# A fused attention and feed-forward kernel: another hand-written order for the first stage, other planned times and SBUF places behind it

## The chip, the cores and the metric

The kernel runs on one core of a Trainium2 chip. The metric is the time of one execution on the device in microseconds; of several runs the median is taken.

## The reference

Attention of 8 batches with 8 heads, 576 positions and 64 values a head. Heads 0 to 3 see the last 32 positions, heads 4 to 7 every fourth of the last 128. Its output is the x of a dense feed-forward network:

```
scores = q @ k.T / 8, masked: rel = pos_q - pos_k
  heads 0-3: 0 <= rel < 32        heads 4-7: 0 <= rel < 128 and rel % 4 == 0
attn = softmax(scores) @ v                      # (8, 8, 576, 64)
x = attn as (4608, 512)                         # 4608 tokens
y = gelu_exact(x @ w_in) @ w_out                # w_in (512, 2048), w_out (2048, 512)
```

Everything is float32 at the inputs and outputs.

## The kernel before

The tokens are worked in chunks of 512: chunk c is the first 512 positions of a batch, and the last 64 positions of all batches make chunk 8. Products are made in parts: a float32 operand is split into a high and a low part, and each product of two operands is three matmuls, so that the weights are unpacked at the start (`split`, `rest`, `high` and `join` of w0 to w15: VectorE and ScalarE make the high and low part of each column block f of the two weight matrices in SBUF, L275 to L312; `mid` is a second way for some of them).

The first stage computes the attention of chunks 0 and 1 and the whole feed-forward network of chunk 0 (`h0` to `h15`: x times w_in and GELU, L689 and L696 to L701; `o0` to `o15`: times w_out, L712) while the weights arrive. The second computes chunks 1 and 2 (`ffn(1, f)`, `ffn(2, f)`, L689 and L712, too), with the weights kept in SBUF. Meanwhile the unpacked weights and sums of them go to DRAM (`keep`, L736, into wd; sums made by GpSimd and VectorE, L831 to L855, into sd). The third stage (from 236 us) takes the other six chunks in pairs; two chunks together take seven block products for eight (Strassen's way, M1 to M7). It reads weights and sums back in pieces of 512 KB through a ring of five places (`ring_load`, L1073), each loaded when TensorE has used the piece before in that place. VectorE and ScalarE make the operands (L962 to L978 for x, L1164 to L1196 for h and GELU) and take the results from PSUM (L1202 to L1277).

The attention of the later chunks lies between the products. For pairs of heads (c, p) the steps are: load of q and k (L338), `scores` on TensorE (L375, L389), the lowest score and its exponent (`lowest_half`, L439 and L441), `softmax` on ScalarE (L510), `norm_half` and `turn_both` on VectorE (L446 to L457), eight small transfers `swap_keys` that move keys between partitions (L465, two for each r of 0 to 3), a load of v (L344), `av_four` on TensorE (L655) and `x_back` on VectorE (L668). The pair (c, 0) carries heads of p 0 and 1, (c, 2) those of p 2 and 3.

Three tables set the order. SCHEDULE is a hand-written list of tokens; each token advances the named piece of work by one instruction on the engine that its letter or its default gives (`:a` ScalarE, `:d` VectorE), and `plan:26` sends out all planned steps with a time below 26. All later work consists of numbered steps with a planned time in units (a product of 6 matmuls is one unit, 1.36 us, in the third stage), to which SHIFTED adds its own number; they are sorted and sent out between the products of TensorE:

```
    def add(at, rank, gen):
        steps.append((round(at + SHIFTED.get(len(steps), 0), 4), rank, len(steps), gen))
...
    def upto(pos):
        nonlocal at
        while at < len(steps) and steps[at][0] < pos - 1e-6:
            at_once(steps[at][3])
            at += 1
```

PLACE_OF names for each tile the SBUF place that it takes (w: 19 places of a weight or 1024 columns, xg: 12, go: 4, sm: 3, st: 5); a tile waits until all users of the place before it are done. Every engine takes its instructions in the order in which they are sent out, and SP issues all transfers, again in that order, so that a transfer whose condition is not met holds those behind it.

The steps that are spoken of: 12 is lowest_half of (2, 0); 60 turn_both of (3, 0), 61 to 64 its swap_keys, 65 its load of v, 66 its av_four; 135 and 300 are av_four of (4, 2) and (6, 0), 323 that of (6, 2); 248 is turn_both of (5, 0), 249 to 252 its swap_keys; 449, 453, 458 and 460 are VectorE's sums of x for one pair of chunks; 789 is a last sum of a result of the pair before, whose outputs are written by step 790; ring load n is step 497 + n. 

Of the kernel before, what the change touches and what calls it, by code (L numbers as in the profile page):

```python
# [116 lines left out]
    xg="""0 1 2 3 4 5 6 7 8 9 10 11 0 1 2 3 9 10 11 0 1 2 3 9 0 1 2 3 9 4 2 5 6 7 8 3 9 4 2 5 6 7 3 9 4 7 3 4 7 8 6 3 4 7 8 10  # L117
11 0 1 5""",
    go="""0 1 2 3 0 1 2 3 0 1 2 3 0 1 2 3 0 1 2 3 0 1 2 0 3 1 2 0 3 1 2 0 3 1 2 0 3 1 2 0 3 0 3 1 2 2 1 3 0 3 0 2 1 2 1 3 0 3 0
# [1363 lines left out]
```

## Time and profile before

| | |
|---|---|
| median of 3 runs | 825.4 us (825.24 to 826.22) |
| the profiled execution | 823.03 us |
| its span, from the first to the last instruction | 821.2 us |
| mean granted TensorE clock | 0.997 |
| TensorE busy | 798.8 us, 97% |
| VectorE busy | 610.8 us, 74% |
| ScalarE busy | 537.9 us, 65% |
| GpSimd busy | 65.0 us, 8% |

A view of the profile shows an execution's instructions on each engine with start and duration, and, for an engine that stood still, the instruction or transfer that released it. A line such as L465 is the line of the kernel that issued it; the names are those of the tiles (ps is PSUM, sm, st and turned are tiles of the softmax, ring the ring of weights). SPq is SP's queue. The line of releasers names the condition that came last by the profile.

### The profile page before, as it was taken

To read this page: it belongs to the slowest core of one execution; us is meant where nothing else is said; L and a number is where in the kernel's file an instruction comes from. 1 tells how busy PE (TensorE), PEld (TensorE's weight loads), DVE (VectorE), ACT (ScalarE), POOL (GpSimd) and SP (SyncE) were. 2 spreads that over 40 slices of the span, in tenths; PEclk is the share of its full clock that TensorE was granted. 3 is DMA by queue.
4 is the path that set the end of the run, shared out by engine and by line. 5 is a ranking of instruction groups with operands and counts; after the bars stand their busy time and mean duration, and the time that the engine had idled before them with its cause. 6 is when DMAs were issued, how large, how long until landed. Compare 5 with 4: busy or idle time off the path is not lost.

```text
span 821.2 us, 19943 instructions
## 1 busy us (share of the span) xinstructions
PE 798.8 (97%) x8354; PEld 652.8 (79%) x8354; DVE 610.8 (74%) x717; ACT 537.9 (65%) x1182; POOL 65.0 (8%) x80
## 2 busy tenths in 40 slices
PE   7899989999999999999999999999999999999997
PEld 5688878888787878888887788888888888888886
DVE  8889865799988879855767698846574987183848
ACT  7588855667677666776566776959775647444452
POOL 2000005633333000000000000000000000000000
PEclk9999999999999999999999999999999999999999
DMA  9998388997989988887987778966576687656564
GB/s 358 416 420 347 122 327 326 349 336 278 302 295 320 285 272 287 267 296 242 335 262 253 214 239 273 341 213 236 159 245 202 192 285 228 202 184 200 188 199 155
DMA packets 132073, 218.61 MB, mean 266 GB/s; under 512 B 7184, under 2 KB 107792, under 8 KB 125584
## 3 DMA queue, kind: packets, MB, share of 16 engines
q1 hardware_dynamic: 131840, 217.21, 77.6%
q8 instruction: 66, 1.08, 0.5%
q14 instruction: 23, 0.19, 0.1%
q10 hardware_dynamic: 144, 0.13, 0.0%
HBM read 167.51 MB, written 42.99 MB: 256 GB/s over the span
## 4 chain that ended last, share of the span: by engine, by line
PE 86%; DVE 5%; DMA 4%; issue 2%; SPq 2%; ACT 1%; DVEq 0%; ACTq 0%
PE ps L1145 62%; PE ps L689 9%; PE ps L712 8%; PE ps L389 3%; PE ps L655 2%; DMA ring<-sd 2%; SPq L465 1%; DMA turned<-turned 1%; DMA raw_qk<-qk 1%; DVE sums L841 1%; DMA v_sb<-v 1%; DVE g L701 1%; PE ps L612 1%; PE ps L601 1%; DVE sums L851 1%
## 5 line engine op out<-in xcount | busy, mean ns | idle before, releaser
L1145 PE MATMUL ps<-g,ring 128*128 128x512 f32 x1170 | 271.5, 391 | 1.6 <-ACT g_value L1178 1.6
L1145 PEld LDWEIGHTS ps<-g,ring 128*128 128x128 f32 x1170 | 218.4, 188 | 49.0 <-issue 2.1
L1145 PE MATMUL ps<-xc_T,ring 128*128 128x512 f32 x672 | 163.2, 391 | 0.0
L1145 PEld LDWEIGHTS ps<-xc_T,ring 128*128 128x128 f32 x672 | 125.5, 188 | 26.7 <-DVE xc_T L970 0.3
L1192 DVE TENSOR_TENSOR g<-g_value,g 128x1024 fp32r<-128x1024 f32 x85 | 103.0, 1220 | 51.6 <-ACT g L1191 51.5
L1191 ACT CAST g<-g_value 128x1024 fp32r<-128x1024 f32 x85 | 88.6, 1049 | 28.4 <-DVE g_value L1193 13.0
L1145 PE MATMUL ps<-xc_B,ring 128*128 128x512 f32 x432 | 106.7, 391 | 0.0
L689 PE MATMUL ps<-x,weight 128*128 128x512 f32 x384 | 94.6, 398 | 2.5 <-DVE weight L191 2.1
L1145 PEld LDWEIGHTS ps<-xc_B,ring 128*128 128x128 f32 x432 | 80.7, 188 | 17.0
L712 PE MATMUL ps<-g,weight 128*128 128x512 f32 x384 | 91.4, 392 | 0.3 <-issue 0.3
L689 PEld LDWEIGHTS ps<-x,weight 128*128 128x128 f32 x384 | 72.3, 191 | 19.0 <-DVE weight L191 2.5
L712 PEld LDWEIGHTS ps<-g,weight 128*128 128x128 f32 x384 | 71.4, 188 | 15.7 <-issue 0.5
L510 ACT ACTIVATE sm<-sm,st 128x64 f32<-128x64 f32 (+1 forms) x224 | 75.8, 341 | 10.1 <-DVE st L441 9.9
L831 POOL TENSOR_TENSOR whole<-weight 128x512 f32<-128x512 f32 x32 | 52.2, 1663 | 67.5 <-DVE sums L841 29.8
L1170 ACT COPY ps<-ps 128x512 f32<-128x512 f32 x28 | 16.0, 571 | 61.3 <-PE ps L1145 55.2
L1212 DVE TENSOR_TENSOR acc_C<-ps,acc_C 128x1024 f32<-128x1024 f32 (+1 forms) x40 | 39.9, 1006 | 16.9 <-PE ps L1145 16.3
L1166 ACT COPY u<-ps 128x512 f32<-128x512 f32 x56 | 32.6, 584 | 20.5 <-PE ps L1145 20.2
L510 ACT ACTIVATION_READ_ACCUMULATOR sm<-sm,st 128x1 f32 x224 | 42.3, 189 | 0.0
L696 ACT ACTIVATE gf<-ps 128x512 f32<-128x512 f32 x32 | 19.1, 597 | 25.6 <-PE ps L689 21.6
L701 DVE TENSOR_TENSOR g<-gf,g 128x512 fp32r<-128x512 f32 x32 | 26.1, 818 | 12.9 <-ACT g L189 12.7
L389 PEld LDWEIGHTS ps<-raw_qk 64*32 64x32 f32 x2304 | 26.3, 110 | 11.5 <-issue 8.7
L1202 ACT COPY ps<-ps 128x512 f32<-128x512 f32 x52 | 28.9, 570 | 9.4 <-PE ps L1145 7.7
(162 smaller groups left out, 959.5 us busy)
## 6 DMA issues: line engine op xcount, KB each, us to landing
ring<-sd SPq DMA_DIRECT2D x112, 512.0 KB, 4.7
ring<-wd SPq DMA_DIRECT2D x84, 512.0 KB, 4.7
v_sb<-v SPq DMA_DIRECT2D x17, 1024.0 KB, 6.2
raw_qk<-qk SPq DMA_DIRECT2D x32, 512.0 KB, 6.5
wd<-weight SPq DMA_DIRECT2D x16, 1024.0 KB, 10.5
sd<-sums SPq DMA_DIRECT2D x16, 1024.0 KB, 6.2
raw_w<-w SPq DMA_DIRECT2D x15, 1024.0 KB, 17.4
mid_w<-w SPq DMA_DIRECT2D x8, 1023.5 KB, 17.4
```

What stands on the lines that cost most here:

```text
L389: nc.tensor.matmul(s.sc[32 * r:32 * r + 32, h, c0:c0 + s.nk], x[:, q0:q0 + 32], x[:, k0:k0 + s.nk], start=s.c > 1, stop=s.c > 1 or u == NU ...
L510: nc.scalar.activation(t, s.sc[:, h, at:at + 2 * KB] if s.c < 2 else t, AF.Exp, bias=st[:, 0], scale=SCALE if s.c < 2 else -1.0, accum_out ...
L689: nc.tensor.matmul(bank, weights[f][:, t, cc * P:(cc + 1) * P], x[:, xx], start=n == 1 and i == 0, stop=n == parts and i == 2)
L701: nc.vector.tensor_sub(g[:, 1], gf, g[:, 0])
L712: nc.tensor.matmul(ps[:, O_BANK.get(c, 0) + d], weights[f][:, t, DM + d * P:DM + (d + 1) * P], gs[f][:, u], start=f == first and n == 0, s ...
L831: nc.gpsimd.tensor_add(to, x, y)
L1145: nc.tensor.matmul(ps[:, bank], lhs, rhs, start=start and i == 0, stop=i == 5, skip_group_check=True)
L1166: nc.scalar.copy(spare_tile[k, i], bank("a", i))
L1191: add(base + t, 4, run("a", lambda k=k, v=v: nc.scalar.copy(operand(k, 0, final), val(v, j))))
L1192: add(base + t1, 4, run("d", lambda k=k, v=v: sub(operand(k, 1, final), val(v, j), operand(k, 0, final))))
L1202: add(base + t, 2, run("a", lambda: nc.scalar.copy(ps[:, to], ps[:, of])))
L1212: plus(to, src, to)
```

## The change

SCHEDULE differs from the token `join12.0` on: the unpacking of weights 12 to 15, the attention of chunk 1, the last blocks of chunk 0 and the writes of the kept weights stand in another order. The numbers of SHIFTED are other ones for most steps, so that 856 of the 1855 steps of the whole plan, tokens and numbered steps together, come at another place in the order. PLACE_OF names another place for 155 of 338 tiles. No instruction is added or removed, and the operands, shapes and engines are the same but for a few copies. The core of the diff, with the lines that hold the steps named above:

```diff
--- before.py
+++ after.py
...
 
...
-    0: 4.6, 1: -52.55, 4: -17.45, 5: -18.9, 6: 9.25, 7: -47.3, 8: -19.75, 9: -0.95, 10: -1.05, 11: -22.65, 12: -32.75, 13: -1.25,
...
-    53: -0.85, 54: -2.65, 55: -4.05, 56: -2.6, 57: -3.7, 58: -1.35, 59: -2.9, 64: -1.05, 65: 5.1, 67: 1, 70: -0.65, 75: 1.25,
...
-    124: 5.7, 125: 9.1, 127: 7.4, 128: 10.5, 129: 10.65, 130: 16.05, 131: 14, 132: 10.5, 133: 10.05, 134: 22, 135: 11.8,
...
-    295: 14.8, 296: 12.15, 297: 10, 298: 8.3, 299: 7.15, 300: 7.25, 301: 20.55, 302: 10.45, 303: -34.15, 304: -2.25, 310: -2.45,
-    317: 5.3, 318: 9.65, 319: 6.15, 320: 5, 321: 9, 322: 6.6, 323: 6.45, 324: 9.25, 325: 10.5, 326: -16.4, 327: 2.55, 328: -6.3,
...
-    432: 1.85, 434: -5, 437: 9.85, 438: 10.55, 440: 9.4, 441: 6.1, 442: 6.2, 448: 11, 449: 14.45, 450: 12.55, 451: 14.9,
-    452: 14.3, 453: 6.3, 454: 6.45, 455: 4.6, 464: 7.2, 465: 10.9, 468: 14.8, 469: 15.95, 470: 16.8, 471: 10.2, 472: 10.15,
...
-    490: 8.25, 491: 2.7, 494: 8.9, 495: 8.45, 496: 4.65, 497: -11.1, 500: 3.65, 501: 4.35, 504: 2.75, 505: 6.65, 506: 6.1,
-    507: 3.45, 508: 6.3, 509: 3.75, 510: 4.3, 511: 1.75, 512: 1.5, 514: 4.05, 515: 3.95, 516: 3.85, 517: 1.7, 520: 5.35,
...
-    788: 40.85, 789: 25.3, 790: 40.4, 795: 2.8, 796: 2.25, 804: 2, 805: 2.85, 810: 2.6, 813: 1.8, 814: 1.55, 815: 2.65, 816: 2.05,
...
+    47: -0.7, 50: -2.6, 51: -2.1, 52: -0.9, 53: -0.7, 54: -2.3, 55: -3.2, 56: -3.3, 57: -4.5, 58: -1, 59: -2.85, 60: -2.65,
+    61: 2.25, 64: -0.65, 65: 0.6, 66: -0.25, 69: -2.15, 70: -0.5, 76: -0.35, 82: 3.45, 83: 5.7, 84: 8.85, 85: 6.2, 86: 6.8,
...
+    130: 17.85, 131: 15.05, 132: 9.85, 133: 8.75, 134: 24.75, 135: 13.6, 136: 13.55, 137: 16.25, 138: -28.05, 139: -301.1,
...
+    293: 10.25, 294: 12.3, 295: 11.4, 296: 15.05, 297: 14.6, 298: 7.95, 299: 8.5, 300: 9.45, 301: 15.9, 302: 20.25, 303: -19.65,
...
+    319: 11.5, 320: 9.9, 321: 8.05, 323: 7.6, 324: 5.3, 325: 8.55, 327: 5.45, 328: 16.6, 329: 10.65, 330: 6.75, 333: 5.75,
...
+    438: 8.65, 439: 11.7, 440: 13, 441: 4.3, 442: 6.35, 443: -2.7, 448: 16.75, 449: 24.85, 450: 12.4, 451: 13, 452: 16.4,
+    458: 8.7, 459: 7.25, 460: 5.7, 461: 5, 462: 4.15, 463: 6.9, 464: 11.25, 465: 12.7, 467: 20.55, 468: 11.8, 469: 16.1,
...
+    502: 0.95, 504: 4.75, 505: 4.55, 506: 3.3, 507: 1.8, 509: 3.75, 510: 5.25, 512: 2.5, 518: 3.9, 519: 5, 520: 6.3, 521: 4.95,
...
-x1.0 x1.1:d x1.1 w15 h8 h8:a join11.1 split10 h8 join12.0 w13 split10*2 join12.1 h9 scores1.2 scores1.3
-high10:a rest10*2 low1.2 low1.2:a o7 h9 exp1.2 split11 h9:d split11 h10 h9 exp1.2 split11 exp1.3 rest11 o8 rest11 exp1.3
-high11:a sums1.2:d sums1.2 o9 split12 h10 join13.0 v1.2 norm1.2:d split12 norm1.3:d split12 turn1.2 turn1.3 h11 h10:a
-rest12 turn1.3:a h10 turn1.2:a high12:d join13.1 rest12 av1.2 h11 split13 mid14 h11:a split13 h12
-h11 join15.0 w14 split13 o10 av1.3 h12 h12:a rest13 join15.1 h12 o11 rest13 high13:a x1.2:a split14 x1.2 x1.3:a keep0
-qk2.2 split14*2 x1.3 h13 qk2.3 plan:26 rest14*2 keep1 keep2 o12 plan:27 high14:d h13 split15 h13:a split15 keep3 h13 h14 plan:28 split15
-rest15*2 o13 plan:29 high15:a keep4 h14 h14:a h15 plan:30 h14 o14 plan:31 h15 h15:a h15 o15 store0.0:d store0.2:a store0.1:a store0.0 store0.2
-store0.3:d store0.3 store0.1 keep5 keep6 keep7
...
+split10 h8 join12.0 h9 w13 split10*2 join12.1 h9 scores1.2 scores1.3 high10:a rest10*2 low1.2 low1.2:a o7 o8 exp1.3
+exp1.2 h9:d split11*3 h9 o9 exp1.3 rest11 exp1.2 h10 sums1.2:d rest11 high11:a join13.1 sums1.2 split12 join13.0 v1.2
+norm1.3:d norm1.2:d h10 split12 turn1.3:a turn1.2 split12 h10:a rest12 turn1.3 high12:d mid14 h10 rest12 split13
+turn1.2:a h11 split13*2 av1.2 h11 keep0 h12 o10 h11 av1.3 rest13 h12 join15.1 w14 join15.0 h12 h11:a h12:a rest13
+high13:a split14 o11 keep1 split14 h13:a x1.2 x1.3:a split14 x1.3 h13 keep3 x1.2:a qk2.2 h13 qk2.3 keep2 rest14 high14:d
+rest14 plan:26 split15 plan:27 split15 o12 h14 h13 split15 plan:28 o13 rest15*2 plan:29 keep4 high15:a h14 h15 h14 h14:a
+h15:a h15 o14 h15 o15 store0.3:d store0.0:d plan:30 store0.0 store0.1 store0.3 store0.2 store0.1:a store0.2:a keep7
+keep6 keep5 plan:31
```

The lines of PLACE_OF differ in the same way in w, xg and go.

## Rows read from the trace of the kernel before

**Rows 1.** The page, part 1: busy us, share of the span, instructions.

```profile
PE 798.8 (97%) x8354; PEld 652.8 (79%) x8354; DVE 610.8 (74%) x717; ACT 537.9 (65%) x1182; POOL 65.0 (8%) x80
```

**Rows 2.** What TensorE waits for: us in total, times, longest.

```profile
PE ps L655 <- DMA turned<-turned: 2.1, 2, 1.6
PE ps L689 <- DVE weight L191: 2.1, 1, 2.1
PE ps L655 <- DMA v_sb<-v: 1.8, 1, 1.8
PE ps L1145 <- ACT g_value L1178: 1.6, 1, 1.6
PE ps L655 <- DMA ring<-sd: 1.3, 1, 1.3
...
PE ps L1145 <- DMA ring<-sd: 1.0, 1, 1.0
...
PE ps L712 <- issue: 0.3, 1, 0.3
```

**Rows 3.** Windows: us, busy of each engine, granted clock, DMA share, GB/s.

```profile
120.00:124.00 4.00, 4.00 (x12) 2.94 (x11) 2.28 (x4) 3.93 (x5) 0.00 (x0) 0.63 1.00 414
...
113.00:200.00 87.00, 84.93 (x1092) 69.35 (x1092) 69.02 (x79) 55.81 (x148) 38.76 (x46) 0.98 0.90 341
...
213.00:217.00 4.00, 3.85 (x138) 3.38 (x139) 4.00 (x4) 1.54 (x2) 2.02 (x2) 1.00 1.05 408
...
240.00:330.00 90.00, 86.97 (x1020) 70.99 (x1008) 77.34 (x86) 64.66 (x134) 6.88 (x4) 1.00 0.90 292
330.00:660.00 330.00, 326.96 (x3359) 268.13 (x3358) 232.64 (x261) 229.41 (x489) 0.00 (x0) 1.00 0.77 249
```

**Rows 4.** Timeline of VectorE, 113 to 121 us: start, us, line, tiles.

```profile
114.60 1.22 DVE L439 SCALAR_TENSOR_TENSOR sm<-ps,masks 128x1024 f32<-128x1024 f32 x1 [2.19 <-PE ps L389]
...
118.86 0.69 DVE L191 CAST weight<-raw_w 128x1024 fp32r<-128x1024 f32 x1
```

**Rows 5.** The chain that ended last: start, us, what.

```profile
100.50 2.94 PE ps L689 x12
...
119.60 4.58 PE ps L689 x12
...
206.51 6.59 DMA v_sb<-v
...
293.86 7.41 DMA ring<-sd
...
345.21 1.56 PE ps L655 x90
```

**Rows 6.** Timeline of SP, the queue that issues the transfers.

```profile
201.44 4.97 SPq L465 DMA_DIRECT2D turned<-turned  x8
...
256.02 0.58 SPq L1073 DMA_DIRECT2D ring<-wd  x1
256.65 0.68 SPq L1073 DMA_DIRECT2D ring<-sd  x1
...
292.50 0.53 SPq L1073 DMA_DIRECT2D ring<-wd  x1
...
338.52 5.01 SPq L465 DMA_DIRECT2D turned<-turned  x8
```

**Rows 7.** Timelines of TensorE (264, 303 us) and VectorE (326, 337 us).

```profile
264.74 1.08 PE L1145 MATMUL ps<-g,ring 128*128 128x512 f32 x4 [1.61 <-ACT g_value L1178]
...
303.04 2.20 PE L1145 MATMUL ps<-g,ring 128*128 128x512 f32 x9
...
326.21 1.29 DVE L1212 TENSOR_TENSOR acc_early<-ps,acc_early 128x512 f32<-128x512 f32 x2 [1.52 <-PE ps L1145]
...
337.21 1.25 DVE L457 STREAM_TRANSPOSE turned<-sm 128x1024 f32<-128x1024 f32 x1
```

**Rows 8.** Transfers: count, KB each, median us from issue to landing.

```profile
ring<-sd SPq DMA_DIRECT2D x112, 512.0 KB, 4.7
```

More of the change, by code (lines that the diff above doesn't have):

```diff
@@ L114 @@
     w="""0 1 2 3 4 5 6 7 8 9 10 11 12 13 14 15 16 17 18 1 3 2 5 6 7 8 9 10 13 11 14 18 16 17 3 2 6 7 9 14 18 11 3 17 10 0 7 17
-18 0 6 7 18 14 2 9 18 0 11 3 14 17 2 3 18 9 0 17 10 11 9 6 3 0 18 7 2 11 4 12 6 9 3 4 18 7 15 11 1 0 4 5 8 7 17 15 12
-14 11 18 6 13 16 12 17 1 11 1 5 16 16 5 17 5 9 11 5 9 10 18 9 0 18 10 11 9 18 0 11 18 0 10 9 5 11 0 10 5 11 18 0 5 10""",
-    xg="""0 1 2 3 4 5 6 7 8 9 10 11 0 1 2 3 9 10 11 0 1 2 3 9 0 1 2 3 9 4 2 5 6 7 8 3 9 4 2 5 6 7 3 9 4 7 3 4 7 8 6 3 4 7 8 10
-11 0 1 5""",
-    go="""0 1 2 3 0 1 2 3 0 1 2 3 0 1 2 3 0 1 2 3 0 1 2 0 3 1 2 0 3 1 2 0 3 1 2 0 3 1 2 0 3 0 3 1 2 2 1 3 0 3 0 2 1 2 1 3 0 3 0
-2 1 2 1 3 0 3 0 2 1 2 1 3 0 3 0 2 1 2 1 3 0 3 0 2 1 2 1 3 0 3 0 2 1""",
+18 0 7 6 14 2 9 18 17 3 11 2 7 14 10 17 11 18 7 2 3 7 0 6 9 18 2 11 4 7 10 12 18 2 0 4 6 9 18 15 11 1 5 8 6 12 4 17 18
+0 10 14 9 13 16 8 12 11 10 13 4 8 8 4 11 8 10 2 8 10 14 2 5 2 14 10 3 5 2 10 3 14 2 3 5 8 10 3 14 8 2 10 3 14 2""",
+    xg="""0 1 2 3 4 5 6 7 8 9 10 11 0 1 2 3 9 10 11 0 1 2 3 9 0 1 2 3 9 4 2 5 6 7 8 3 9 4 2 5 6 7 8 3 9 7 8 3 9 6 2 8 3 9 6 10
+11 0 1 4""",
+    go="""0 1 2 3 0 1 2 3 0 1 2 3 0 1 2 3 0 1 2 3 0 2 1 3 0 2 1 3 0 2 1 3 0 2 1 3 0 2 1 3 0 3 0 2 1 2 1 3 0 3 0 2 1 2 1 3 0 0 3
+2 1 1 2 0 3 0 3 1 2 1 2 0 3 3 0 1 2 1 2 0 3 0 3 1 2 1 2 0 3 0 3 1 2""",
     sm="""0 1 2 0 1 2 1 2 0 1 2 0 1 2 0 1 2 0 1 2 0""",
@@ L126 @@
 low0.0 high0.0:a rest0.0 v0.0 rest0.0 low0.0:a scores0.2 exp0.0 low0.1 split0.1 fill split0.1 low0.1:a scores0.3
-sums0.0:a split0.1 exp0.1 mid1 sums0.0 low0.2 exp0.1 low0.2:d norm0.0:d exp0.2 turn0.0 w1 sums0.1:d fill*3 sums0.1 norm0.1:d
-low0.3 exp0.2 low0.3:d split0.1 turn0.1 half0.0.1:d half0.0.0:d v0.2 half0.1.1:a half0.1.0:a fill*2
-sums0.2:d sums0.2 norm0.2:d exp0.3 mid2 av0.0 turn0.2 exp0.3 rest0.1*2 high0.1:d w2 x0.0:a x0.1:a sums0.3:d sums0.3 norm0.3:d
-x0.0 x0.1 h0.0 turn0.3 h0.1 half0.2.0:a half0.2.1:a half0.3.1:a half0.3.0:a split1*3 qk1.0 av0.2 high1:a rest1*2 qk1.1 h1.0 h1.1
@@ L131 @@
-x0.2:a x0.3:a x0.2 x0.3 h0.2 h0.3 split2 h0 mid3 h1.2 w3 h1.3 scores1.0 burn*45 h0:a split2*2 high2:a rest2*2 h0 h1 h1:a h2 scores1.1
-split3 w4 mid5 split3 h1 o0 split3 rest3 h2 mid4 h2:a rest3 low1.0 low1.0:a
-exp1.0 o1 high3:d w5 exp1.0 h2 h3 split4 exp1.1 mid6 split4*2 exp1.1 o2 rest4 high4:a w6 rest4 h3
-split5*2 h4 w7 h3:a split5 sums1.0:a h3 high5:a rest5 o3 w8 rest5 h4 h4:a split6 join7.0 h4 w11 h5 split6 sums1.0
-join7.1 split6 norm1.0:d high6:a w9 o4 rest6*2 h5 h5:a split7 join8.0 mid9 h5 h6 split7 norm1.1:a split7 v1.0 join8.1
@@ L136 @@
-rest7 turn1.0 turn1.1 rest7 o5 high7:a split8 h6 qk1.2 split8 h6:a split8 turn1.0:a w10 h7 turn1.1:a h6 join11.0 rest8
-high8:a rest8 qk2.0 av1.0 split9 h7 split9 qk1.3 join10.0 split9 h8 av1.1 w12 h7:a h7 high9:a rest9 join10.1 x1.0:a qk2.1 rest9 o6
-x1.0 x1.1:d x1.1 w15 h8 h8:a join11.1 split10 h8 join12.0 w13 split10*2 join12.1 h9 scores1.2 scores1.3
-high10:a rest10*2 low1.2 low1.2:a o7 h9 exp1.2 split11 h9:d split11 h10 h9 exp1.2 split11 exp1.3 rest11 o8 rest11 exp1.3
-high11:a sums1.2:d sums1.2 o9 split12 h10 join13.0 v1.2 norm1.2:d split12 norm1.3:d split12 turn1.2 turn1.3 h11 h10:a
@@ L145 @@
-store0.3:d store0.3 store0.1 keep5 keep6 keep7
+sums0.0:a split0.1 exp0.1 mid1 sums0.0 low0.2 exp0.1 low0.2:d norm0.0:d exp0.2 turn0.0 w1 sums0.1:d fill*3 sums0.1
+norm0.1:d low0.3 exp0.2 low0.3:d split0.1 turn0.1 half0.0.1:d half0.0.0:d v0.2 half0.1.1:a half0.1.0:a fill*2 sums0.2:d
+sums0.2 norm0.2:d exp0.3 mid2 av0.0 turn0.2 exp0.3 rest0.1*2 high0.1:d w2 x0.0:a x0.1:a sums0.3:d sums0.3 norm0.3:d x0.0
+x0.1 h0.0 turn0.3 h0.1 half0.2.0:a half0.2.1:a half0.3.1:a half0.3.0:a split1*3 qk1.0 av0.2 high1:a rest1*2 qk1.1 h1.0
@@ new lines @@
+h1.1 x0.2:a x0.3:a x0.2 x0.3 h0.2 h0.3 split2 h0 mid3 h1.2 w3 h1.3 scores1.0 burn*45 h0:a split2*2 high2:a rest2*2 h0 h1
+h1:a h2 scores1.1 split3 w4 mid5 split3 h1 o0 split3 rest3 h2 mid4 h2:a rest3 low1.0 low1.0:a exp1.0 o1 high3:d w5
+exp1.0 h2 h3 split4 exp1.1 mid6 split4*2 exp1.1 o2 rest4 high4:a w6 rest4 h3 split5*2 h4 w7 h3:a split5 sums1.0:a h3
+high5:a rest5 o3 w8 rest5 h4 h4:a split6 join7.0 h4 w11 h5 split6 sums1.0 join7.1 split6 norm1.0:d high6:a w9 o4 rest6*2
+h5 h5:a split7 join8.0 mid9 h5 h6 split7 norm1.1:a split7 v1.0 join8.1 rest7 turn1.0 turn1.1 rest7 o5 high7:a split8 h6
@@ new lines @@
+qk1.2 split8 h6:a split8 turn1.0:a w10 h7 turn1.1:a h6 join11.0 rest8 high8:a rest8 qk2.0 av1.0 split9 h7 split9 qk1.3
+join10.0 split9 h8 av1.1 w12 h7:a h7 high9:a rest9 join10.1 x1.0:a qk2.1 rest9 o6 x1.0 x1.1:d x1.1 w15 h8 h8:a join11.1
+split10 h8 join12.0 h9 w13 split10*2 join12.1 h9 scores1.2 scores1.3 high10:a rest10*2 low1.2 low1.2:a o7 o8 exp1.3
+exp1.2 h9:d split11*3 h9 o9 exp1.3 rest11 exp1.2 h10 sums1.2:d rest11 high11:a join13.1 sums1.2 split12 join13.0 v1.2
+norm1.3:d norm1.2:d h10 split12 turn1.3:a turn1.2 split12 h10:a rest12 turn1.3 high12:d mid14 h10 rest12 split13
```

101 rows, old and new, of the table SHIFTED are left out of this document.

## The prediction

> **What bounds the kernel now.** I read the busy times first. TensorE has work in 798.8 us of a span of 821.2 us, and VectorE, the next, in 74% [rows 1]. No other engine can be the bound on average, so nothing that this change does to them pays unless it shortens the 22.4 us in which TensorE stands still (821.2 - 798.8). Second, the list of what TensorE waits for [rows 2]. A good part of it is the start of the kernel (attention of chunk 0, up to 80 us), which the new order does not touch, and some of it lies behind the last product. The rest, in time of the span, is seven stalls: one wait of 2.1 us for a weight, 2.1 us in two waits for turned keys, 1.8 us for a load of v, 1.6 us put down to a g value, 1.3 us and 1.0 us for loads into the ring, and 0.3 us of issue. Together they are 2.1 + 2.1 + 1.8 + 1.6 + 1.3 + 1.0 + 0.3 = 10.2 us, and this is what the change can take, with what follows from them. Third, the windows: in both long stretches up to 330 us, 113 to 200 and 240 to 330, the DMA engines are busy 0.90 of the time [rows 3], so transfers there cannot simply be moved ahead. Fourth, the chain and the timelines of the queues, to see who made each of the seven late.
>
> **The weight (117.5 us).** In VectorE's order the lowest-score step of the pair (2,0), step 12 (L439, L441), stands ahead of `rest14` (L300, L302), and it needs scores that end just before 114.60; VectorE is idle for 2.19 us before it and then needs until 118.86 to reach `high14`, for which `h14` waits [rows 4]. After the stall the granted clock is 0.63 over 120 to 124 us, between its two levels of 1.2 and 2.4 GHz [rows 3], and the 12 matmuls of `h14` take 4.58 us where the 12 of another product behind an attention block take 2.94 [rows 5]: 1.64 us more. In the new SCHEDULE `rest14 high14 rest14` stand ahead of `plan:26`, which means ahead of step 12 for VectorE, and weight 14 goes to a place that split14 itself frees. Then VectorE uses its idle 2.19 us and weight 14 is there some 2 us before TensorE wants it: -2.1 - 1.64 = -3.7 us. In exchange `high15` now runs on ScalarE behind seven pieces of softmax; adding up that queue I find it about 0.35 us late for `h15`: +0.35.
>
> The Trainium skill, page "TensorE: Matmul & The Clock Gate", section on HAM oscillation, says that a TensorE left waiting between bursts of matmuls starts the next burst at the lower clock, and pays for it at every such wait. If that held for each of the stalls of 1 us and more here, another five times 1.64 us would come back, and the time below would be 8.2 us lower. The trace doesn't agree: the clock is 1.00 in the 4 us behind the 1.8 us wait, and 1.00 over 240 to 330 us, where three more stalls lie [rows 3]. So I take this gain once.
>
> **v of pair (3,0) (211 us).** The eight swaps of keys (L465) wait for the turn, go out at 201.44 over 4.97 us, and the load of v stands behind them; it goes out at 206.51 and takes 6.59 us [rows 5, 6]. In the new numbers load_v (step 65) loses 4.5 units and stands ahead of the swaps, and the turn (step 60) loses 2.65. The matmuls that need it (step 66) come 0.25 units earlier, 2.72 us on TensorE, with over 2 us of room left: -1.8.
>
> **The ring (263, 293 us) and the keys (306, 432, 471 us).** Loads of the ring stand in SP's queue in pairs that are out of order: load 10 waits for TensorE and is issued at 256.02, load 9 behind it at 256.65 [rows 6], though the place of load 9 was free earlier. With the 7.41 us of a neighbour [rows 5] it lands at about 264.1, close to where the stall ends that the list puts down to the g value (264.74, [rows 7]). Steps 506 and 507 change from 6.1 and 3.45 to 3.3 and 1.8, which sets load 9 ahead: -1.6. Loads 19 and 20 (steps 516, 517) are the same, from 3.85 and 1.7 to none: -1.0. The matmuls on (4,2) and (6,0) (steps 135, 300) are moved back by two products, 2.72 us, the latter's turn comes some 2.5 us earlier, and (6,2) (step 323) moves back by one product while its swaps go ahead of the next ring load: -2.1 - 1.3. The 0.3 us of issue I count as gone with the order around it: -0.3. Sum of what goes: 3.7 + 1.8 + 1.6 + 1.0 + 2.1 + 1.3 + 0.3 = 11.8 us.
>
> **What the new order adds.** No instruction is added or removed, except that by the order of exponential and GELU on ScalarE I count 38 table loads for 42; ScalarE waits for others at most of these points, so I price that at nothing. The matmuls of the products are the same and in nearly the same order. What can cost is a step that comes too late.
>
> First, 131 to 240 us. The lowest and turn steps of chunk 2 are re-sorted among VectorE's sums for the ring. VectorE is busy 69.0 of the 87 us to 200 us [rows 3], so most slips are absorbed. Of several places the margin by my sums is 0 to 2 us (matmuls on (2,2), the x of chunk 2, (2,0) whose turn now waits for a place that GpSimd frees). Below: 0. Above: four places late by one operation of 1.22 us [rows 4], 4.9. I take one operation: +1.2.
>
> Second, 303 us. Ring load 21 was issued at 292.50 for matmuls at 303.04, 10.5 us ahead [rows 6, 7]; step 518 gets 3.9 units, and load 21 now stands behind four swaps that wait for a turn; its lead comes to 5.6 us. A neighbour took 7.41 us to land, the median of ring loads is 4.7 [rows 5, 8]. So 0 to 1.8 us; I take +1.0.
>
> Third, 345 us. Eight swaps for (5,0) start at 338.52, behind the turn (1.25 us from 337.21), over 5.01 us, and the matmuls on them began at 345.21, with 0.2 us to spare [rows 5 to 7]. Step 789 loses its 25.3 units and is now in VectorE's queue ahead of this turn, steps 449 and 458 gain units and are too, while steps 453 and 460 are out of the way: three operations for two between VectorE's last wait (326.21, [rows 7]) and the turn. One operation of some 1.15 us, less the 0.2: +0.95. If none of VectorE's idle time before 326 absorbs anything, three operations are late, and the cost is 3.5; if the swaps land faster, 0.
>
> Fourth, ring load 133 (643 us) gets behind four swaps in the same way, with a lead of 4.4 us against the median of 4.7: +0.5, between 0 and 1.5. And eight further places, from 328 to 737 us, where VectorE or ScalarE have up to 1 us more in their queue than before; both idle a quarter of the time or more, so +0.7 over all, between 0 and 3.
>
> Sum of additions: 0.35 + 1.2 + 1.0 + 0.95 + 0.5 + 0.7 = 4.7 us. Net 11.8 - 4.7 = 7.1 us.
>
> **The rivals.** (a) The DMA engines take it back. With seven stalls gone TensorE is up to 10 us ahead in the third stage, and every load is wanted that much earlier, while the DMA engines are busy 0.90 of the time up to there [rows 3]. Ten loads that miss by 0.7 us each give back all of it: 825. For it speaks that the ring loads near 290 us took 7.41 where the median is 4.7; against it, that after 330 us the share falls to 0.77, and that a load's issue waits for TensorE to free its place, so that both move together. The Trainium skill, page "DMA: Bandwidth & Descriptors", section on issuing engines, says that transfers run on the same 16 engines and interleave whoever issues them, so a load that is moved ahead delays another. The row of 0.90 agrees; by that rule alone the two ring stalls and the one for v would only change place, and 4.4 us of the gain would be gone.
>
> (b) Nearly full gain: if landings are at their medians, the additions shrink to under 2.5 us. 825.4 - 9.3 to 825.4 - 11.8: 813.6 to 816.1.
>
> (c) Slower. The keys for (5,0) are the one place where one queue holds up everything: SP's. If the turn is late by three operations and two outputs of the finished pair ahead of the swaps wait as well, all loads behind them on SP are late too: ring loads 36 to 39, each wanted 2.7 us after the other. It costs more than the 11.8 us only if the swaps go out about 15 us late (11.8 plus the other additions of 3.8, less 0.2 of slack), that is, if step 789 waits for a place or an operand that comes that late; at 17 us the time is about 827. I see no such operand in the numbers of the change.
>
> (d) The order of SP could be right and the first term wrong: if `h14` still waits for its weight, 3.7 us less gain, 822.
>
> **How the numbers follow.** The profiled execution took 823.03 us, of which 821.2 are span; the median of the runs is 825.4, 2.4 above it. Seen from the profiled one the sum is 823.03 - 7.1 = 815.9; on the median's footing, which is what will be compared, 825.4 - 7.1 = 818.3. A difference of 0.2% is 1.65 us, about what a measurement of this kernel can tell from none. My chances: the forecast (816.2 to 821.5) 0.56; (b) 0.15; (d) and the like, a smaller gain of 1.7 to 3.9 us, 0.11; (a) within 1.65 us of before 0.10; slower, by (c) or a sum of small stalls, 0.08. Faster: 0.56 + 0.15 + 0.11 = 0.82. For the range I leave out the last 0.08 and about half of (a) above, and the lowest half of (b) below: 814.8 to 824.6.
>
> **What would show it.** In the new profile: VectorE's `rest14` before L439 and no wait of TensorE for L191 near 117 us, with a clock of 1.00 over 120 to 124; the load of v ahead of L465's eight; ring loads from sd in the order of their use, and no wait at 263 and 293; new waits, if any, for turned keys near 340, and for the ring near 300 and 635. TensorE's idle time should fall from 22.4 to about 17 us. I am wrong if waits for DMA sum to as much as before, if the clock drops at another place, or if a wait of more than 3 us stands anywhere behind 113 us.

## The result and the profile after

The changed kernel takes 815.7 us in the median (815.06 to 818.61, 4 runs) where the kernel before took 825.32. The ratio is 0.9896, with a 95% interval of 0.9862 to 0.9929, so it is faster by 0.7 to 1.4%. A second measurement, beside experiments, gave 816.18 us and 0.9913 (0.988 to 0.9946). Over both, 12 runs of the changed kernel have a median of 815.7 us, and the 79 runs of the kernel before that were taken beside the experiments one of 822.8: 7.1 us. (Each measurement by itself gives 9.6 and 6.6 us.)

The profiled execution of the changed kernel is the slowest of its four runs, 818.61 us with a span of 816.7. Its busy times, against [rows 1]:

```profile
PE 801.0 (98%) x8354; PEld 653.2 (80%) x8354; DVE 609.3 (75%) x717; ACT 533.7 (65%) x1178; POOL 62.6 (8%) x80
```

TensorE now stands still for 816.7 - 801.0 = 15.7 us instead of 22.4. What it still waits for (us in total, times, longest), against [rows 2]:

```profile
PE ps L1146 <- DMA ring<-wd: 2.6, 1, 2.6
...
PE ps L390 <- DMA raw_qk<-qk: 1.8, 4, 0.6
...
PE ps L656 <- DMA turned<-turned: 0.4, 1, 0.4
```

All seven stalls of [rows 2] are gone or small: no weight, no v, no g value, 0.4 us of turned keys. What is left of any size behind 113 us is one new wait of 2.6 us for a load into the ring, beside 0.4 us of the waits for raw_qk and 0.2 us for ScalarE. The windows, against [rows 3] (us, busy time of PE, PEld, DVE, ACT, POOL with counts, granted clock, DMA share, GB/s):

```profile
113.00:200.00 87.00, 86.46 (x1103) 70.40 (x1103) 67.53 (x81) 58.24 (x151) 35.82 (x46) 1.00 0.85 316
...
240.00:330.00 90.00, 90.00 (x1000) 73.48 (x999) 82.36 (x88) 66.62 (x138) 5.91 (x4) 1.00 0.92 306
330.00:660.00 330.00, 327.08 (x3346) 267.85 (x3345) 230.21 (x258) 222.66 (x473) 0.00 (x0) 0.99 0.77 245
...
120.00:124.00 4.00, 3.97 (x17) 2.95 (x17) 1.97 (x3) 3.98 (x14) 1.50 (x8) 1.00 1.02 430
...
506.00:510.00 4.00, 2.66 (x6) 2.15 (x7) 2.70 (x5) 0.00 (x0) 0.00 (x0) 0.61 1.07 379
...
545.00:550.00 5.00, 5.00 (x173) 4.42 (x166) 1.40 (x2) 3.10 (x6) 0.00 (x0) 0.78 0.39 118
```

TensorE is busy in all of the 90 us from 240 to 330 where it was in 86.97, and VectorE does 82.36 us of work there for 77.34, although the DMA engines are as full as before (0.92 for 0.90). From 120 to 124 us the clock is 1.00 instead of 0.63. But it is low at two new places: behind the new wait (0.61 over 506 to 510 us) and from 545 us on, where TensorE had no idle time at all. This execution is 3.5 us above the fastest run, whose mean clock was 0.999 where this one's was 0.996; (1 - clock) times the span is 0.8 us there and 3.3 us here, so the clock is 2.5 of the 3.5 us.

The place of the weight, on VectorE and then ScalarE (start, us, engine, line, operation, tiles), against [rows 4]:

```profile
112.31 0.68 DVE L301 TENSOR_SCALAR spare<-raw_w 128x1024 uint32<-128x1024 uint32 x1
112.91 0.68 DVE L192 CAST weight<-raw_w 128x1024 fp32r<-128x1024 f32 x1
113.51 1.22 DVE L303 SCALAR_TENSOR_TENSOR weight<-raw_w,spare 128x1024 fp32r<-128x1024 uint32 x1
114.64 1.22 DVE L440 SCALAR_TENSOR_TENSOR sm<-ps,masks 128x1024 f32<-128x1024 f32 x1
...
121.82 1.10 ACT L190 CAST weight<-raw_w 128x1024 fp32r<-128x1024 f32 x1
122.94 1.28 ACT L697 ACT_TABLE_LOAD   x1
```

`rest14`, `high14` and the second `rest14` (L301, L192, L303) run from 112.31 to 114.73, and the lowest-score step (L440) only then, at nearly the same time as before. `high15` ends on ScalarE at 122.92. The chain, against [rows 5]:

```profile
117.51 2.72 PE ps L690 x12
...
122.97 3.01 PE ps L690 x12
...
507.34 13.90 PE ps L1146 x54
```

`h14` (117.51) and `h15` (122.97) begin without a wait in the list; `high15` ended 0.05 us before `h15` began. The scores of (2,2) and (2,3), which stood at 124 us between the last products of chunk 0, are now at 134.32. SP's queue, against [rows 6]:

```profile
493.99 5.02 SPq L466 DMA_DIRECT2D turned<-turned  x8
...
499.69 0.58 SPq L1074 DMA_DIRECT2D ring<-wd  x1
...
330.81 5.03 SPq L466 DMA_DIRECT2D turned<-turned  x8
```

The swaps for (5,0) begin at 330.81 and the matmuls on them at 337.66, 6.9 us later; it was 6.7 before, and there is no wait. The new wait stands at 507.34: eight swaps for (8,0) go out from 493.99 on, and the ring load behind them only at 499.69; the chain has 7.51 us for it.

### The profile page after: what moved, and what is told of

Read it like the earlier page. It is cut to its first block, busy times and chain, and to the rows that moved or that the text cites. A ratio compares the mean times of both kernels' runs of the same rounds, so it can differ in the third digit from the quotient of the medians.

```text
span 816.7 us, 19941 instructions
## 1 busy us (share of the span) xinstructions
PE 801.0 (98%) x8354; PEld 653.2 (80%) x8354; DVE 609.3 (75%) x717; ACT 533.7 (65%) x1178; POOL 62.6 (8%) x80
## 4 chain that ended last, share of the span: by engine, by line
PE 84%; DVE 7%; DMA 4%; ACT 2%; issue 1%; SPq 1%; DVEq 0%; ACTq 0%
PE ps L1146 62%; PE ps L690 8%; PE ps L713 7%; PE ps L390 3%; DMA raw_qk<-qk 2%; PE ps L656 2%; ACT sm L511 1%; DMA v_sb<-v 1%; DVE sums L842 1%; DMA ring<-wd 1%; DVE sums L852 1%; PE ps L613 1%; PE ps L602 1%; SPq L466 1%; DMA turned<-turned 1%
## 5 line engine op out<-in xcount | busy, mean ns | idle before, releaser
L1175 DVE TENSOR_TENSOR g_value<-ps,u 128x512 f32<-128x512 f32 x28 | 19.2, 688 | 25.4 <-PE ps L1146 23.6
```

## The experiments

The twelve runs were taken in three groups, each on a chip of its own and beside the kernel before: `e1` to `e4` (before: 824.12 us), `a_again` and `u1` to `u3` (822.76), `e6` to `e8` and `u4` (822.33). Between groups the ratios are compared. `e1` to `e3` and `e6` to `e8` make a part of the change in the kernel before; `u1` to `u4` undo one part of it in the changed kernel; `e4_fix` goes beyond it. Each profile is one execution. Numbers in the diffs are entries of SHIFTED. Changes of the places that only follow from a moved step are left out of the diffs.

**The ring loads alone, in the kernel before (`e1_ring`).**

```diff
-    506: 6.1, 507: 3.45, 516: 3.85, 517: 1.7
+    506: 3.3, 507: 1.8
```

> The kernel before with four numbers changed, so that ring load 9 stands ahead of load 10 and load 19 ahead of load 20 in SP's queue. Theory of the order in the queue: TensorE's waits of 1.6 us near 263 and 1.0 us near 293 are gone and nothing takes their place but some tenths at the keys of (4,2) near 306: 1.6 to 2.6 us faster than before. Rival, that the DMA engines set the pace there: a later load or transfer misses instead, the waits for DMA keep their sum and the time stays within 0.8 us of before.

Measured: 828.67 us (822.6 to 832.39), ratio 1.0058 (1.0033 to 1.0083): slower, which neither theory had expected. TensorE's waits in its profile (start, us, tiles, and in brackets idle time and releaser) and, behind the last "...", SP's queue:

```profile
267.00 12.64 PE L1145 MATMUL ps<-g,ring 128*128 128x512 f32 x48 [1.99 <-ACT g L1191]
...
294.86 1.61 PE L1145 MATMUL ps<-xc_T,ring 128*128 128x512 f32 x6 [1.26 <-DMA ring<-sd]
...
257.93 0.58 SPq L1073 DMA_DIRECT2D ring<-wd  x1
258.56 0.67 SPq L1073 DMA_DIRECT2D ring<-sd  x1
```

The edit does more than it was meant to. By the planned times load 9 is now ahead of load 10, but both are also ahead of load 8 (step 505: 6.65 here, 4.55 in the change), and load 19 is ahead of 17 and 18 (steps 514 and 515: 4.05 and 3.95 here, none in the change). TensorE needs these loads in the order of their numbers, which the change gives them. So the transfer at 258.56, behind load 10 (257.93), is load 8; it takes 8.1 us to land, to 266.7, and TensorE goes on at 267.00. The list names a cast of g on ScalarE instead, but under `e7_ringkeys`, which has the same four numbers, TensorE goes on while that cast still runs. The wait at 294.86 is for load 17, sent out behind 19. The keys of (4,2) cost 1.93 us for 0.46. This run therefore does not show what loads in the order of their use would bring.

**The weight alone, in the kernel before (`e2_weight`).**

```diff
-qk2.2 split14*2 x1.3 h13 qk2.3 plan:26 rest14*2 keep1 keep2 o12 plan:27 high14:d h13 split15
+qk2.2 split14*2 x1.3 h13 qk2.3 rest14 high14:d rest14 plan:26 keep1 keep2 o12 plan:27 h13 split15
```

> The kernel before with rest14, high14, rest14 ahead of the lowest-score step of (2,0) in VectorE's queue, and SBUF places 0 and 6 exchanged from there on. Theory: the wait of 2.1 us for weight 14 is gone, the granted clock over 120 to 124 us is 1.00, and the gain is 2.1 + 1.6 = 3.7 us. Rival A: the clock is low there for another reason than the stall, and only 2.1 us come back. Rival B: the wait moves to weight 15 or to the scores behind, and less than 1 us comes back.

Measured: 822.22 us, ratio 0.9974 (0.9955 to 0.9993), 2.1 us faster: the size that rival A gives, but by the mechanism of rival B. ScalarE and, from 122.56 on, TensorE in its profile:

```profile
119.96 1.28 ACT L696 ACT_TABLE_LOAD   x1
...
122.52 1.28 ACT L510 ACT_TABLE_LOAD   x1
...
126.49 1.11 ACT L189 CAST weight<-raw_w 128x1024 fp32r<-128x1024 f32 x1
...
122.56 3.33 PE L712 MATMUL ps<-g,weight 128*128 128x512 f32 x12 [0.89 <-ACT g L189]
127.65 3.06 PE L689 MATMUL ps<-x,weight 128*128 128x512 f32 x12 [1.77 <-ACT weight L189]
```

The wait for weight 14 is gone, but what follows is held by ScalarE: it loads its table for GELU at 119.96, loads the one for the exponential again at 122.52, does eight pieces of softmax, and casts `high15` at 126.49, for which TensorE waits 1.77 us. It also waits 0.89 us for a g. In these stretches the clock is 1.00, although 1.77 us is nearly as long a wait as the 2.07 us of before.

This profile also bears on the ring. Its loads are those of before, and near 264 us TensorE waits 0.95 us, again with ScalarE's g value named:

```profile
263.61 2.56 PE L1145 MATMUL ps<-g,ring 128*128 128x512 f32 x10 [0.95 <-ACT g_value L1178]
```

It goes on at 263.61, while load 9, sent out at 256.13, takes 8.6 us and lands only at 264.7. So it is not load 9 that TensorE waits for here.

**The keys and the load of v, in the kernel before (`e3_keys`).**

```diff
-    65: 5.1, 135: 11.8, 300: 7.25, 323: 6.45
+    65: 0.6, 135: 13.6, 300: 9.45, 323: 7.6
```

> The kernel before with the load of v for (3,0) ahead of the swaps of keys, and the matmuls of (4,2), (6,0) and (6,2) moved back by two, two and one products. Theory of single late transfers: the waits near 211 (1.8 us), 306 and 432 (2.1 us together) and 471 (1.3 us) go, 5.2 us faster than before. Rival, that transfers are late because the DMA engines are full: products behind these places wait for ring loads instead, and less than 2.5 us comes back.

Measured: 834.54 us, ratio 1.0124 (1.0104 to 1.0145), 10 us slower. SP's queue and what TensorE waits for:

```profile
200.26 0.33 SPq L344 DMA_DIRECT2D v_sb<-v  x1
...
211.65 5.51 SPq L465 DMA_DIRECT2D turned<-turned  x8
```

```profile
PE ps L712 <- DVE g L701: 6.2, 1, 6.2
PE ps L389 <- DVE xn L668: 3.0, 1, 3.0
```

The load of v was sent out so early that it stood at the head of SP's queue until its place came free at 200.26. Five other transfers stood behind it, loads of q and k among them, and the swaps that began at 201.44 [rows 6] now begin at 211.65; TensorE waited 6.2 + 3.0 = 9.2 us for VectorE. That is my edit, not the change, which gives this tile another place and sends the load out at 187.25. Behind 330 us this kernel has no wait: TensorE is busy in all of 330 to 660 us. The waits at 432 and 471 did go with matmuls that come later.

**One number more, in the changed kernel (`e4_fix`).**

```diff
-    588: 5.45
+    588: 1.0
```

> The changed kernel with one number more changed: step 588, ring load 91, from 5.45 to 1.0, so that it stands ahead of the eight swaps of keys for (8,0). Theory: the wait of 2.6 us near 507 in the changed kernel is load 91 standing behind the swaps in SP's queue; it goes, and the time is 2.5 us under the changed kernel's 815.7, some 813 us, 12 under before. Rival, the landing itself is slow there because all 16 DMA engines are busy: the load goes out 5 us earlier but the swaps land later, and TensorE waits for turned keys instead; less than 1 us under 815.7.

Measured: 813.87 us (812.8 to 815.03), ratio 0.9875 (0.9854 to 0.9896). SP's queue:

```profile
490.35 4.39 SPq L1074 DMA_DIRECT2D ring<-wd  x2
494.78 5.06 SPq L466 DMA_DIRECT2D turned<-turned  x8
```

The second of the two ring loads at 490.35 is now ahead of the swaps, which begin 0.8 us later, and there is no wait near 507. This is the lowest median here; its interval overlaps with the changed kernel's, so that only the lost wait, not its size in the time, is settled.

**The changed kernel again (`a_again`).**

> The changed kernel itself once more, on the same chip as the three kernels that undo one part of it. Every theory expects 0.9896 of the time before within 0.3%, and in the profile the wait of 2.6 us for a ring load near 507 us.

Measured: 816.18 us, 0.9913 (0.988 to 0.9946). The wait near 507 us:

```profile
506.48 12.51 PE L1146 MATMUL ps<-g,ring 128*128 128x512 f32 x54 [1.47 <-DMA ring<-wd]
```

It is there, but 1.47 us long, and the clock stays at 1.00 over 506 to 510 us; this profiled execution took 813.96 us.

**The ring loads undone, in the changed kernel (`u1_ring`).**

```diff
-    506: 3.3, 507: 1.8
+    506: 6.1, 507: 3.45, 516: 3.85, 517: 1.7
```

> The changed kernel with the four numbers of ring loads 9, 10, 19 and 20 as before, so that both pairs stand in SP's queue in the order of before. The prediction's theory: the waits of 1.6 us near 263 and 1.0 us near 293 come back, 2.6 us slower than the changed kernel. Rival, that the profile's list was right to name ScalarE's g value at 263: only the 1.0 us comes back, or less. Second rival, that these loads have room in the new order: nothing comes back.

Measured: 819.79 us, ratio 0.9963 (0.9939 to 0.9987), 3.6 us over the changed kernel beside it. The chain near 263 us, and the window behind the wait:

```profile
258.47 1.08 SPq L1074
259.60 7.66 DMA ring<-sd
267.40 12.84 PE ps L1146 x48
```

```profile
267.00:271.00 4.00, 3.60 (x9) 2.92 (x10) 0.00 (x0) 0.00 (x0) 0.00 (x0) 0.59 0.93 357
```

Load 9 goes out behind loads 11 and 10, of which load 11 waits for TensorE until 258.06, and lands after 7.66 us: TensorE waits 3.93 us, and its clock is 0.59 over 267 to 271. The wait is longer than before because load 11, whose number (step 508) the edit leaves, stood behind load 9 in the kernel before. That the order in the queue sets when a load lands holds at this place; the 3.6 us are the price of this order, not of that of before. At 293 there is no wait.

**The weight undone, in the changed kernel (`u2_weight`).**

```diff
-high13:a split14 o11 keep1 split14 h13:a x1.2 x1.3:a split14 x1.3 h13 keep3 x1.2:a qk2.2 h13 qk2.3 keep2 rest14 high14:d
-rest14 plan:26 split15 plan:27 split15 o12 h14 h13 split15 plan:28 o13 rest15*2 plan:29 keep4 high15:a h14 h15 h14 h14:a
+high13:a split14 o11 keep1 split14 h13:a x1.2 x1.3:a split14 x1.3 h13 keep3 x1.2:a qk2.2 h13 qk2.3 keep2 plan:26 rest14 high14:d
+rest14 split15 plan:27 split15 o12 h14 h13 split15 plan:28 o13 rest15*2 plan:29 keep4 high15:a h14 h15 h14 h14:a
```

> The changed kernel with the lowest-score step of (2,0) ahead of rest14 and high14 on VectorE, as before. Theory: the step ends at 117.1, high14 some 1.3 us later, so TensorE waits some 1.9 us for weight 14 near 117.5, and its clock falls behind the wait: 1.9 + 1.6 = 3.5 us slower than the changed kernel. Rival: the clock stays at 1.00 and only the wait counts, 1.9 us. Second rival: ScalarE is then ahead with the softmax and weight 15 no longer late, and under 1 us is lost.

Measured: 816.55 us, ratio 0.9917 (0.9889 to 0.9946), 0.4 us over the changed kernel. TensorE near 117 us:

```profile
118.49 0.49 PE L690 MATMUL ps<-x,weight 128*128 128x512 f32 x1 [0.81 <-DVE weight L192]
119.62 2.79 PE L690 MATMUL ps<-x,weight 128*128 128x512 f32 x11 [0.64 <-DVE weight L303]
```

Two waits of 0.81 and 0.64 us: the first matmul can go when `high14` is there and the others only after `rest14`. The span of this profile is 814.5 us, 2.5 above the other's; the clock is 1.00 over 120 to 124 us. In the medians nearly nothing of it is seen.

**The load of v undone, in the changed kernel (`u3_v`).**

```diff
-    65: 0.6
+    65: 5.1
```

> The changed kernel with the load of v for (3,0) behind six of the eight swaps of keys, as before. Theory: the load goes out some 5 us later, lands after 6.6 us, and TensorE waits up to 1.8 us for it at the matmuls of (3,0). Rival: in the new order the turn for (3,0) comes so much earlier that the load has room behind the swaps as well, and under 0.5 us is lost.

Measured: 814.24 us, ratio 0.9885 (0.9855 to 0.9916), no slower than the changed kernel. There is no wait at the matmuls of (3,0). The rival is right.

**Both weights, in the kernel before (`e6_weights`).** The edit of `e2_weight`, and:

```diff
-... h13 split15 h13:a split15 keep3 h13 h14 plan:28 split15
-rest15*2 o13 plan:29 high15:a keep4 ...
+... h13 split15*2 h13:a split15 high15:a keep3 h13 h14 plan:28
+rest15*2 o13 plan:29 keep4 ...
```

> The kernel before with rest14 and high14 ahead of the lowest-score step, as in the first edit of the weight, and with the third split15 ahead of the g of block 13 and high15 ahead of the second softmax on ScalarE. Theory: the wait of 1.8 us for weight 15, which took the place of the one for weight 14 in the first edit, was high15 standing behind a table load and eight pieces of softmax; it goes, and the gain against before is 3 to 4 us instead of 2. Rival: h15 then waits for rest15 on VectorE or TensorE waits at the next place, and the gain stays at 2 us.

Measured: 823.51 us, ratio 1.0017 (0.9998 to 1.0036): no gain. TensorE:

```profile
122.26 3.31 PE L712 MATMUL ps<-g,weight 128*128 128x512 f32 x12 [0.91 <-ACT g L189]
...
129.94 7.65 PE L712 MATMUL ps<-g,weight 128*128 128x512 f32 x24 [1.65 <-ACT g L189]
```

Neither weight is late, and TensorE waits 0.91 and 1.65 us for g, which ScalarE makes. The queue of ScalarE, not a weight, holds this stretch.

**The ring loads and later matmuls, in the kernel before (`e7_ringkeys`).**

```diff
-    135: 11.8, 300: 7.25, 323: 6.45, 506: 6.1, 507: 3.45, 516: 3.85, 517: 1.7
+    135: 13.6, 300: 9.45, 323: 7.6, 506: 3.3, 507: 1.8
```

> The kernel before with the four ring loads in order of use and the matmuls of (4,2), (6,0) and (6,2) moved back by two, two and one products. Theory: ring order alone lost time because the keys of (4,2) and (6,0) then came late; with the matmuls later the two together gain 2 to 4 us. Rival: in the order of before the operands of ScalarE near 264 us set the end, not the load, and each wait that goes returns at the next place: within 1.5 us of before, or slower.

Measured: 823.49 us, ratio 1.0013 (0.9993 to 1.0033): the rival in the time. TensorE waits 1.43 and 1.25 us for ring loads and 1.53 us for a g from VectorE; the last lines are the transfer at 256.57 and who waited for it (us, times):

```profile
264.60 11.08 PE L1145 MATMUL ps<-g,ring 128*128 128x512 f32 x48 [1.43 <-DMA ring<-sd]
...
290.87 1.62 PE L1145 MATMUL ps<-xc_T,ring 128*128 128x512 f32 x6 [1.25 <-DMA ring<-sd]
...
313.32 9.43 PE L1145 MATMUL ps<-g,ring 128*128 128x512 f32 x40 [1.53 <-DVE g L1192]
...
L1073 SPq DMA_DIRECT2D ring<-sd x1: 700/700/700, 256.6 to 256.6; - x1
...
  PE ps L1145: 1.4, 1
```

That transfer is load 8, directly behind load 10, as in `e1_ring`; it takes 7.8 us to land, and TensorE goes on at 264.60, before ScalarE's cast (263.94 to 264.99) is done. At 290.87 it is load 17, behind load 19. These two waits are made by the edit. The waits for keys at 432 and 471 us are gone, and the one for VectorE's g at 313 is new.

**Both of these, in the kernel before (`e8_all`: the edits of `e6_weights` and of `e7_ringkeys`, without the load of v).**

> The kernel before with both: the weights 14 and 15 in time, the ring loads in order and the three groups of matmuls later. Theory of single places: the gains add up, 5 to 8 us faster than before, most of what the change brings with 856 steps moved. Rival: between 200 and 480 us the order of VectorE's and ScalarE's queues sets the end, so these few numbers bring no more than the weights alone, 2 to 4 us.

Measured: 824.45 us, ratio 1.0022 (1.0003 to 1.004): no gain from the two together. Some of TensorE's larger waits:

```profile
264.72 12.78 PE L1145 MATMUL ps<-g,ring 128*128 128x512 f32 x48 [1.94 <-ACT g L1191]
...
315.56 10.98 PE L1145 MATMUL ps<-g,ring 128*128 128x512 f32 x40 [1.23 <-DVE g L1192]
```

The two waits for ScalarE's g of `e6_weights` are there again (0.88 and 1.67 us), and so are those of `e7_ringkeys`: at 264.72 load 8 had landed only at 264.3 (sent out at 256.32, 8.0 us to land), though the list names ScalarE's cast, and 1.67 us are for load 17 at 293. So where the weight had been waited for TensorE now waits for ScalarE, and a wait for VectorE's g is new; the waits at the ring come from the edit's own order. The sum of the single places is not tested by this run, as the ring was not put in the change's order and the load of v (1.6 us here) was left.

**The keys undone, in the changed kernel (`u4_keys`).**

```diff
-    135: 13.6, 323: 7.6
+    135: 11.8, 323: 6.45
```

> The changed kernel with the matmuls of (4,2) two products and those of (6,2) one product earlier, as before. Theory: their turned keys are then late by up to 0.5 and 1.3 us, and up to 1.8 us is lost against the changed kernel. Rival: in the new order the turns and swaps come early enough, and under 0.5 us is lost.

Measured: 820.92 us, ratio 0.9979 (0.9962 to 0.9996), where the changed kernel's was 0.9913 on another chip: some 5 us slower. SP's queue, TensorE, and the window from there:

```profile
293.58 2.41 SPq L466 DMA_DIRECT2D turned<-turned  x4
296.03 0.59 SPq L345 DMA_DIRECT2D v_sb<-v  x1
...
303.15 1.89 PE L656 MATMUL ps<-v_sb,turned 64*32 64x64 f32 x128 [2.58 <-DMA v_sb<-v]
```

```profile
303.00:307.00 4.00, 3.85 (x133) 3.32 (x134) 0.10 (x1) 3.95 (x13) 0.00 (x0) 0.59 1.09 351
```

The place is the one that the theory named, but not the transfer: what is late for (4,2) is its load of v, which goes out behind the swaps at 296.03 and takes 6.98 us; TensorE waits 2.58 us, and the clock is 0.59 over the next 4 us. At (6,2) there is no wait. This profile and that of `u1_ring` also have a wait of 1.10 us for VectorE's g near 202 us, ahead of what either edit moves, which stands in neither profile of the changed kernel: waits differ between executions, and a profile alone does not give a price.

## Why the prediction was right

The direction was right, and so was the size on average (7.1 us, against 7.1 in the pooled medians). The 815.7 us of the first measurement lie in the range of rival (b), 0.5 us under the forecast's; by the ratio, 0.9896 times 825.4, it is 816.8 and in the forecast's. That the size came so near is in part luck, as the parts show.

- **What bounds the kernel.** Right: TensorE's idle time fell by 6.7 us in the profiled execution, to 15.7 (about 17 was expected). Of the 10.2 us of stalls listed none is left but 0.4 us at the keys; with 2.6 us at the ring, 0.4 of the 1.8 at raw_qk and 0.2, 3.6 us of waits stand behind 113 us now.
- **That a stall's length is what its repair gives.** This step held for the whole and failed for the weight. Put into the kernel before, the repair of weight 14 gave 2.1 us, and that of both weights none: ScalarE was next. Undone in the changed kernel, the weight cost 0.4 us and v none, ring and keys 3.6 and some 5. For the ring the kernel before gives no price, as my edits there moved loads behind their turn. No kernel made from the one before had the 90 us from 240 to 330 without a wait; which of the 856 moved steps are needed for it, and whether SCHEDULE, SHIFTED or PLACE_OF alone would do, was not tried.
- **The weight, 3.7 us.** Too large: 2.1 alone, 0.4 undone. The wait was rightly read, but ScalarE's softmax and its table loads are next in line, which I had priced at nothing (42 loads for 38). In the changed kernel `high15` is ahead of the GELU, and the scores of (2,2) and (2,3) moved from 124 to 134 us; which of the two lets `h15` go wasn't tried alone. The 0.35 us expected for it did not come: TensorE was busy with the product before until `high15` was there. The 1.64 us of clock do not belong to this wait. `e3_keys` and `e7_ringkeys` keep it, with 2.07 and 2.09 us, and their clock is 1.00 over 120 to 124 us; `h14` takes 3.02 and 3.06 us there, against 4.58 in the profile of before. So the clock fell behind this wait in some executions and not in others. The line of `e7_ringkeys`:

```profile
119.36 3.06 PE L689 MATMUL ps<-x,weight 128*128 128x512 f32 x12 [2.09 <-DVE weight L191]
```

- **v, 1.8 us.** The wait went, but not by the load's step: behind the swaps it is in time as well (`u3_v`). The turn that comes earlier is left as the cause, by exclusion only.
- **The ring at 263 us.** My reading that load 9 was the releaser is not borne out: in `e2_weight`, with the loads of before, TensorE went on 1.1 us before load 9 landed. The list, which names ScalarE's g value, is nearer, though this had ended at 263.9 and TensorE went on at 264.74; what held it in between stays open. What took the 1.6 us away in the changed kernel was therefore not tried alone. That a load behind others in SP's queue can cost this place more, 3.9 us, `u1_ring` shows.
- **The keys.** The places were right, and the waits at 432 and 471 us go with matmuls that come later (`e7_ringkeys`). At 306 it is the load of v that needs the two products (`u4_keys`).
- **The additions, 4.7 us.** Near in sum (3.6) by luck, and wrong in place. Ring load 21, the swaps for (5,0) and ring load 133 cost nothing; the turn of (5,0) ended 7.8 us earlier than before, where TensorE was 7.6 us ahead, and VectorE's wait of 1.52 us at 326.21 [rows 7] has no counterpart. The 2.6 us came at load 91, which I passed over; `e4_fix` shows that it stood behind the swaps for (8,0).
- **Rival (a)** is not what happened: with the DMA engines as full as before, 0.92 for 0.90 over 240 to 330 us, the loads came in time. What I had drawn from the Trainium skill's page "DMA: Bandwidth & Descriptors", section on issuing engines, is not borne out: loads that are moved ahead did not merely exchange their delays. That was my inference; that transfers share the engines is not put in doubt.
- **Rival (c)** was added up wrongly: the other additions of 3.8 us shorten the lateness that it needs, 11.8 - 3.8 + 0.2 = 8.2 us and not 15. It did not come about.
- **The signs.** One sign that I had set for being wrong did come: the clock dropped at other places, 506 and 545 us, in the first profile of the changed kernel, though not in the second. The waits for DMA behind 113 us fell from 6.2 to 3.4 us, and none is over 3 us.

The clock may be the rest. The mean granted clock of the 79 runs of before is 0.9963, that of 12 runs of the changed kernel 0.9986; (1 - clock) times the time is 3.1 us for 1.2. By this estimate 1.9 us of the 6.5 us between the means (823.0 and 816.6) are clock and 4.6 us waits; the 6.7 us of idle time that the profiles lost do not fit it closely, so the split is rough. That the 1.9 is close to the 1.64 at one place is chance.

## What to carry to other kernels

In a schedule where several queues run close to one another, the sum of the stalls on the bounding engine says what a new order can give (10.2 us were listed here, and the idle time fell by 6.7), but a single stall's repair gives at most the distance to the next queue (at weight 14 ScalarE was next); look up who is second at each place before pricing it. Undo a part in the faster kernel, too: there the other queues have room, and the part shows its price. Take over every step whose place hangs on the part that you move: two loads put ahead of the one that is needed first made waits of their own. And hold the releaser that a list names against the time at which it ended. A transfer that waits for its place or its data at the head of a queue holds all that stand behind it: read each stall of a load from the line that is issued just ahead of it.

## What was not expected of the hardware

- The clock behind a wait, between its levels of 1.2 GHz (0.50) and 2.4 GHz (1.00). In some executions it was 0.63 and 0.61 over 4 us behind waits of 2.07 and 2.56 us and 0.59 behind 2.58 and 3.93 us, but it was 1.00 behind waits of 1.47, 1.77 and 1.80 us. The length does not decide it: behind the same wait for weight 14 (2.07 to 2.09 us) it was 0.63 in the profile of before, 0.61 in `e1_ring` and 1.00 in `e3_keys` and `e7_ringkeys`; it was 0.62 over the 4 us behind 1.23 us at 315.56 in `e8_all`, and 1.00 behind 3.00 us at 233.27 in `e3_keys`. Where it fell behind weight 14, the 12 matmuls took 4.58 and 4.23 us, where not, 3.02 and 3.06, so that such a wait costs 1.2 to 1.6 us more than itself. What the prediction took from the Trainium skill's page "TensorE: Matmul & The Clock Gate", section on HAM oscillation, that each such wait is paid for twice, holds for some of these waits and not for others; the page tells it of bursts of matmuls that are shorter than the waits between them, not of single waits in dense work.
- The clock also fell without a wait, to 0.78 over 545 to 550 us of the changed kernel's profile, behind 192 matmuls of 32x32; in a second profile it was 1.00 there. Part of the spread of the runs of one kernel goes with such falls: over the 79 runs of before a mean clock that is lower by 0.001 goes with 0.8 us, which is 37% of the variance of their times.
